# Weight pairs in arrival order for the first two x tiles, and two column halves side by side on one stationary operand

## The chip, the cores and the metric

The kernel runs on one core of one Trainium2 chip. The metric is the time of one execution in device microseconds (us). Before the change the median was 496.4 us in three runs.

## The reference

Two attention blocks read the same x (2048 rows, 1024 columns, bf16) and are mixed by a gate for each row. Block A is linear attention, block B attends to 8 positions, each 2 apart.

```
g = sigmoid((x * gate_w).sum(-1))
A: phi(t) = where(t > 0, t + 1, exp(t)) + 1e-6          # 32 heads of 32
   kv = sum_s phi(k) v ;  z = sum_s phi(k) ;  o = phi(q) kv / (phi(q) z + 1e-6) ;  a = o @ A_wo
B: softmax over offsets 0, 2, .. 14 of q.k * 32**-0.5 ;  o = attn v ;  b = o @ B_wo
out = g * a + (1 - g) * b
```

The kernel computes block A's kv through G = x^T phi(k): the V projection of block A is never made. It goes through these stages, in this order on TensorE (PE): warm-up, transposes of the first two x tiles, key projection with phi (`pk_ps`), G (`g_ps`), KV and z (`kv_ps`), V of block B with q of block A (`p_ps`), k and q of block B with its attention (`kq_ps`), the rest of q of block A with the last attention (`q_ps`), the output (`d_ps`). PE's order is fixed by the program; the other engines are scheduled by the toolchain.

## The kernel before

The start. The first two tiles of x are loaded as whole rows by the ACT queue, the first half of the key weights in four parts by the sync queue (SP). The other 14 tiles are transposed by the DMA on their way in.

```python
load_rows(nc.scalar, 0, 1)
load_rows(nc.scalar, 1, 2)
WkA = load_w("WkA", A_wqkv, D, "wa", parts=4, only=(0,))
for t in range(2, NB):
    nc.sync.dma_start_transpose(out=xT[:, :, t * P:(t + 1) * P], in_=rows(x, t * P, (t + 1) * P))
# ... other loads, masks ...
for i in range(5):                       # warm-up: 20 matmuls of 128 columns
    warm = ps_1.tile([P, 512], F32, name="warm", tag="p1")
    for j in range(4):
        nc.tensor.matmul(warm[:, j * P:(j + 1) * P], lhsT=onesb[:], rhs=onesb[:], start=True, stop=True)
for t in range(2):
    tp = ps_1.tile([P, KT, P], BF16, name="xt_ps", tag="p1")
    for kt in range(KT):
        nc.tensor.transpose(out=tp[:, kt, :], in_=xrow[:, t, kt * P:(kt + 1) * P], identity=ident[:])
    nc.vector.tensor_copy(out=xT[:, 0:4, t * P:(t + 1) * P], in_=tp[:, 0:4, :])
    nc.scalar.copy(out=xT[:, 4:8, t * P:(t + 1) * P], in_=tp[:, 4:8, :])
for half in range(2):
    for t in range(NB):
        pj = ps_1.tile([P, 512], F32, name="pk_ps", tag="p1")
        for kt in range(KT):
            nc.tensor.matmul(pj[:], lhsT=xT[:, kt, t * P:(t + 1) * P], rhs=WkA[half][:, kt, :], ...)
        phi(pk[:, t, half * 512:(half + 1) * 512], pj)
```

G, V, q and the output all have this shape: one half of 512 columns is finished before the other begins, and the stationary operand (`lhsT`) is loaded again for the second half.

```python
for half in range(2):                    # G; V, q and output likewise
    for kt in range(KT):
        pj = ps_1.tile([P, 512], F32, name="g_ps", tag="p1")
        for t in range(NB):
            nc.tensor.matmul(pj[:], lhsT=xrow[:, t, kt * P:(kt + 1) * P],
                             rhs=pk[:, t, half * 512:(half + 1) * 512], ...)
        nc.scalar.copy(out=g_[:, kt, :], in_=pj[:])
for c in range(KT):                      # KV: the first one needs G[0][:, 0..7, :]
    for kt in range(KT):
        nc.tensor.matmul(kvp[:], lhsT=WvA[c // 4][:, kt, ...], rhs=G[c // 4][:, kt, ...], ...)
```

The attention writes `Ob`, of which there are two buffers, and a transposing DMA empties it. The output of tile 0 uses banks of the attention's PSUM pools, tiles 1 to 15 use a pool that takes over those banks.

```python
Ob = small.tile([P, 4, 4, Dh], BF16, name="Ob", tag="Ob")      # pool of 2 buffers
# ...
interleave(list(out_units(0, bank8)), carry)                   # tile 0: banks of ps_o and ps_pj
with ExitStack() as s3:
    ps_3 = s3.enter_context(tc.tile_pool(name="ps_3", bufs=6, space=bass.MemoryType.PSUM))
    for t in range(1, NB):                                     # tiles 1 to 15
        ...
```

Of the kernel before, what the change touches and what calls it, by code (L numbers as in the profile page):

```python
# [8 lines left out]
ACT = mybir.ActivationFunctionType  # L9
ALU = mybir.AluOpType  # L10
BF16 = mybir.dt.bfloat16
# [3 lines left out]
P = 128  # L15
# [26 lines left out]
def kernel(  # L42
# [38 lines left out]

    def load_w(name, src, col0, tag, parts=1, only=(0, 1)):
        halves = []
        for h in only:
            w = wpool.tile([P, KT, 512], BF16, name=f"{name}{h}", tag=tag)
            c0 = col0 + h * 512
            n = KT // parts
            for i in range(parts):
                nc.sync.dma_start(
                    out=w[:, i * n:(i + 1) * n, :],  # L90
                    in_=src[i * n * P:(i + 1) * n * P, c0:c0 + 512].rearrange("(kt p) n -> p kt n", p=P))
            halves.append(w)
        return halves
# [4 lines left out]
    def load_rows(eng, t0, t1):  # L98
        eng.dma_start(out=xrow[:, t0:t1, :], in_=rows(x, t0 * P, t1 * P).rearrange("(t p) d -> p t d", p=P))

    load_rows(nc.scalar, 0, 1)
    load_rows(nc.scalar, 1, 2)
    WkA = load_w("WkA", A_wqkv, D, "wa", parts=4, only=(0,))
    for t in range(2, NB):
# [40 lines left out]
    def phi(dst, pj):  # L145
        e = work.tile([P, 512], F32, name="e", tag="e")
        nc.scalar.activation(out=e[:], in_=pj[:], func=ACT.Exp)  # L147
        nc.vector.tensor_scalar(out=e[:], in0=e[:], scalar1=1.0, scalar2=1e-6, op0=ALU.min, op1=ALU.add)  # L148
        nc.vector.scalar_tensor_tensor(out=dst, in0=pj[:], scalar=0.0, in1=e[:], op0=ALU.max, op1=ALU.add)

    with tc.manual_schedule(engines={PE}):

        with ExitStack() as s1:
# [4 lines left out]
            for i in range(5):  # L158
                warm = ps_1.tile([P, 512], F32, name="warm", tag="p1")
                for j in range(4):  # L160
                    nc.tensor.matmul(warm[:, j * P:(j + 1) * P], lhsT=onesb[:], rhs=onesb[:], start=True, stop=True)
            for t in range(2):
                tp = ps_1.tile([P, KT, P], BF16, name="xt_ps", tag="p1")
                for kt in range(KT):
                    nc.tensor.transpose(out=tp[:, kt, :], in_=xrow[:, t, kt * P:(kt + 1) * P], identity=ident[:])
                nc.vector.tensor_copy(out=xT[:, 0:4, t * P:(t + 1) * P], in_=tp[:, 0:4, :])
                nc.scalar.copy(out=xT[:, 4:8, t * P:(t + 1) * P], in_=tp[:, 4:8, :])

            s1.enter_context(tc.manual_schedule(engines={DVE}))
            pk = big.tile([P, NB, D], BF16, name="pk", tag="pkO")  # L170
            for half in range(2):
                for t in range(NB):
                    pj = ps_1.tile([P, 512], F32, name="pk_ps", tag="p1")
                    for kt in range(KT):
                        nc.tensor.matmul(pj[:], lhsT=xT[:, kt, t * P:(t + 1) * P], rhs=WkA[half][:, kt, :],  # L175
                                         start=(kt == 0), stop=(kt == KT - 1))
                    phi(pk[:, t, half * 512:(half + 1) * 512], pj)
            zacc = junk.tile([P, D], F32, name="zacc", tag="zacc")
            gw_row = junk.tile([P, D], BF16, name="gw_row", tag="gw")
            nc.gpsimd.dma_start(out=gw_row[:], in_=gate_w.partition_broadcast(P))  # L180
            zhl = junk.tile([P, 2, D], BF16, name="zhl", tag="zhl")
# [8 lines left out]

            G = []
            for half in range(2):
                g_ = kq.tile([P, KT, 512], BF16, name=f"G{half}", tag="kq")
                G.append(g_)
                for kt in range(KT):
                    pj = ps_1.tile([P, 512], F32, name="g_ps", tag="p1")
                    for t in range(NB):
                        nc.tensor.matmul(pj[:], lhsT=xrow[:, t, kt * P:(kt + 1) * P],  # L198
                                         rhs=pk[:, t, half * 512:(half + 1) * 512],
                                         start=(t == 0), stop=(t == NB - 1))  # L200
                    nc.scalar.copy(out=g_[:, kt, :], in_=pj[:])
                    side(half * 8 + kt)

# [48 lines left out]

            def v_units(t):
                def mm(half, kt, st):
                    if kt == 0:
                        st["pj"] = bank1()
                    nc.tensor.matmul(st["pj"][:], lhsT=xT[:, kt, t * P:(t + 1) * P], rhs=WvB[half][:, kt, :],  # L257
                                     start=(kt == 0), stop=(kt == KT - 1))
                    if kt < KT - 1:
                        return  # L260
                    v = Vst[t % 2]
                    nc.scalar.copy(out=v[:, half * 16:(half + 1) * 16, 0:Dh],  # L262
                                   in_=st["pj"][:].rearrange("p (h e) -> p h e", h=16))
                    if half == 1:
                        par, j = divmod(t, 8)

                        n = 128 - 16 * j
                        nc.sync.dma_start(out=V[16 * j:128, par * 9 + j], in_=v[0:n])
                        nc.sync.dma_start(out=V[0:16 * (j + 1), par * 9 + j + 1], in_=v[128 - 16 * (j + 1):128])
                for half in range(2):  # L270
                    st = {}
                    for kt in range(KT):
                        yield lambda half=half, kt=kt, st=st: mm(half, kt, st)

            def normalize(t, pq, pn, prod):
# [10 lines left out]

            def qa_units(t, bank, evacuate):
                def mm(half, kt, st):
                    if kt == 0:
                        st["pj"] = bank()  # L290
                    nc.tensor.matmul(st["pj"][:], lhsT=xT[:, kt, t * P:(t + 1) * P], rhs=WqA[half][:, kt, :],  # L291
                                     start=(kt == 0), stop=(kt == KT - 1))
                    if kt == KT - 1:
                        evacuate(t, half, st["pj"])
                for half in range(2):
                    st = {}
                    for kt in range(KT):
                        yield lambda half=half, kt=kt, st=st: mm(half, kt, st)

            def qa_finish(t, half, pj):  # L300
# [5 lines left out]

            units = [u for t in range(4) for u in v_units(t)]
            interleave(units, [(4 + 8 * c, w2_event(c)) for c in range(KT)])
            for t in range(12):
                for u in v_units(4 + t):  # L310
                    u()
                for u in qa_units(t, bank1, qa_finish):
                    u()
# [3 lines left out]
        with ExitStack() as s2:  # L317
# [125 lines left out]
            def out_units(tb, bank):  # L443
                def mm(c0, n, side, c, st):
                    if side == 0 and c == 0:
                        st["ps"] = bank()
                    if side == 0:
                        lhsT, W = (pqT[0][:, c, tb * P:(tb + 1) * P] if tb < 4 else
                                   pqT[1][:, c, (tb - 4) * P:(tb - 3) * P]), WoA
                    else:  # L450
                        lhsT, W = OBT[:, c, tb * P:(tb + 1) * P], WoB
                    nc.tensor.matmul(st["ps"][:, 0:n], lhsT=lhsT, rhs=W[c0 // 512][:, c, c0 % 512:c0 % 512 + n],  # L452
                                     start=(side == 0 and c == 0), stop=(side == 1 and c == KT - 1))
                    if side == 0 or c < KT - 1:
                        return
                    osb = work.tile([P, 512], BF16, name="osb", tag="e")
                    nc.scalar.activation(out=osb[:, 0:n], in_=st["ps"][:, 0:n], func=ACT.Copy,  # L457
                                         scale=omg[:, tb:tb + 1])
                    nc.sync.dma_start(out=rows(out2, tb * P, (tb + 1) * P)[:, c0:c0 + n], in_=osb[:, 0:n])
                parts = [(0, 512), (512, 512)] if tb < NB - 1 else [(0, 512), (512, 256), (768, 256)]  # L460
                for c0, n in parts:
                    st = {}
                    for side in range(2):
                        for c in range(KT):
                            yield lambda c0=c0, n=n, side=side, c=c, st=st: mm(c0, n, side, c, st)

# [8 lines left out]
            ev = carry + attention_events(KT - 1, prev, CUTS3, 3, 17)  # L475
            interleave([u for t in range(12, 16) for u in qa_units(t, bank8, qa_keep)], [e for e in ev if e[0] < 64])
            carry = [(p - 64, f) for p, f in ev if p >= 64]
# [46 lines left out]
```

## Time and profile before

| | before |
|---|---|
| median of six runs | 496.32 us (495.89 to 496.88) |
| span of the profiled run | 493.9 us |
| PE busy | 481.6 us, 98% |
| chain of waits, share of PE | 96% |

The first fence shows the busy line of the kernel before: engine, busy us (share of the span), number of instructions. PEld is the weight load of TensorE, which overlaps PE.

```profile
PE 481.6 (98%) x3276; PEld 230.1 (47%) x3336; DVE 283.4 (57%) x550; ACT 182.0 (37%) x281; POOL 8.6 (2%) x29
```

PE is all but always busy, so only what moves PE counts. The next question is whether weight loads cost PE time. The kernel before has one place where two matmuls in a row share a stationary operand, KVT with the two halves of WoA. This is its group (line, engine, operation, number, duration of one in ns, first and last start):

```profile
L246 PEld LDWEIGHTS <-KVT x16: 97/98/98, 123.0 to 138.3; 128*128 128x128 bf16 x16
L246 PE MATMUL p_ps<-WoA_106,KVT x8: 379/379/380, 123.2 to 138.3; 128*128 128x512 bf16 x8
L246 PE MATMUL p_ps<-WoA_108,KVT x8: 379/379/379, 123.4 to 138.5; 128*128 128x512 bf16 x8
```

There are 16 loads for 16 matmuls: a shared operand is loaded twice all the same. 379 ns is the length of one matmul, not its cost: the starts in a stream are 216 ns apart. The G stage shows it without counting records: 256 matmuls take 55.25 us, 215.8 ns each, with a load of 98 ns hidden beneath each.

The timeline of PE at the start (start us, length us, what, how many, in brackets the idle time before it and what ended it):

```profile
2.70 0.74 PE L161 MATMUL warm<-onesb 128*128 128x128 bf16 x5
4.57 1.04 PE L165 MATMUL xt_ps<-ident,xrow 128*128 128x128 bf16 x8 [1.13 <-DMA xrow<-in_A_x_dram]
5.88 1.03 PE L165 MATMUL xt_ps<-ident,xrow 128*128 128x128 bf16 x8 [0.27 <-DMA xrow<-in_A_x_dram]
6.71 5.59 PE L175 MATMUL pk_ps<-WkA_77,xT 128*128 128x512 bf16 x21
```

PE waits for the two tiles of x and then runs. The record of starts has the first key matmuls 427 ns apart, the later ones 216: the clock was at half until 8.06 us. The last view is of PE's waits (who waited for what, us in total, times, longest):

```profile
PE oB_4252 L390 <- DVE Ob L396: 1.5, 1, 1.5
PE xt_ps L165 <- DMA xrow<-in_A_x_dram: 1.4, 2, 1.1
PE kq_ps L334 <- issue: 1.3, 8, 0.2
PE warm L161 <- DVE onesb L119: 1.1, 1, 1.1
PE oB_4202 L390 <- DVE Ob L396: 0.5, 1, 0.5
```

### The profile page before, as it was taken

Reading aid. Unit: us, or ns where it says so; the run is one execution under the profiler, and the core shown is the slowest. Engines: PE = TensorE matmul, PEld = TensorE weight load, DVE = VectorE, ACT = ScalarE, POOL = GpSimd, SP = SyncE. Lnnn points to the kernel's source line nnn. Section 1 sums busy time; section 2 is a strip of 40 time slices with the busy share of each in tenths; the row PEclk is TensorE's granted clock in tenths of the full one; section 3 lists DMA queues with packets and bytes.
Section 4 is the critical chain, followed back from the end, with each engine's and each line's share of the span. In section 5 each row is a group of like instructions: output and inputs, shape, how many; then the busy total and the mean of one; then the engine's idle time right before and its main releaser. Section 6 shows DMA issues by size and latency. Waiting matters only on the chain.

```text
span 493.9 us, 8164 instructions
## 1 busy us (share of the span) xinstructions
PE 481.6 (98%) x3276; PEld 230.1 (47%) x3336; DVE 283.4 (57%) x550; ACT 182.0 (37%) x281; POOL 8.6 (2%) x29
## 2 busy tenths in 40 slices
PE   7999999999999999999999999999998999999997
PEld 4444444446444444444444444544444444444444
DVE  2666699921329999996567676767655596000000
ACT  2333311112543333331555655565564323112121
POOL 4000000001100000000000000000000000000000
PEclk9999999999999999999999999999999999999999
DMA  8999920002422122244011141111172843110101
GB/s 232 163 317 361 345 95 0 1 0 68 152 75 70 74 88 92 94 145 139 11 33 29 27 119 38 29 28 34 31 175 54 209 86 82 36 42 33 43 33 42
DMA packets 78069, 46.03 MB, mean 93 GB/s; under 512 B 51472, under 2 KB 72080, under 8 KB 78032
## 3 DMA queue, kind: packets, MB, share of 16 engines
q1 hardware_dynamic: 77664, 44.73, 32.9%
q10 hardware_dynamic: 288, 0.52, 0.4%
q8 instruction: 26, 0.43, 0.4%
q0 software_dynamic: 80, 0.26, 0.2%
q14 instruction: 11, 0.09, 0.1%
HBM read 21.23 MB, written 7.34 MB: 58 GB/s over the span
## 4 chain that ended last, share of the span: by engine, by line
PE 96%; DMA 2%; issue 1%; DVE 0%; ACT 0%; SPq 0%; ACTq 0%; DVEq 0%
PE kq_ps L334 22%; PE d_ps L452 21%; PE pk_ps L175 11%; PE g_ps L198 11%; PE p_ps L257 11%; PE p_ps L291 8%; PE q_ps L291 1%; DMA OBT<-Ob 1%; DMA xrow<-in_A_x_dram 1%; PE kv_ps L216 1%; PE q_ps_4367 L452 1%; PE p_ps L246 1%; PE q_ps L452 1%; PE q_ps_4147 L291 0%; PE q_ps_4248 L291 0%
## 5 line engine op out<-in xcount | busy, mean ns | idle before, releaser
L198 PE MATMUL g_ps<-pk,xrow 128*128 128x512 bf16 x251 | 55.2, 379 | 0.3
L457 ACT ACTIVATE osb<-d_ps,omg 128x512 bf16<-128x512 f32 (+1 forms) x31 | 20.9, 673 | 77.0 <-PE d_ps L452 72.5
L148 DVE TENSOR_SCALAR e<-e 128x512 f32<-128x512 f32 x64 | 27.2, 425 | 36.0 <-ACT e L147 35.8
L175 PEld LDWEIGHTS <-xT 128*128 128x128 bf16 x256 | 25.3, 99 | 30.4 <-issue 0.6
L452 PEld LDWEIGHTS <-OBT 128*128 128x128 bf16 x264 | 25.8, 98 | 29.2
L198 PEld LDWEIGHTS <-xrow 128*128 128x128 bf16 x256 | 25.0, 98 | 30.2
L257 PEld LDWEIGHTS <-xT 128*128 128x128 bf16 x256 | 25.0, 98 | 30.2
L291 PEld LDWEIGHTS <-xT 128*128 128x128 bf16 x256 | 24.2, 98 | 28.0
L373 DVE TENSOR_TENSOR PT_1878<-PT_1878,mask 128x672 bf16<-128x672 bf16 (+3 forms) x42 | 23.6, 571 | 17.0 <-ACT PT_1878 L371 16.7
L334 PE MATMUL kq_ps<-xT,WqB_1861 128*128 128x512 bf16 x120 | 31.8, 379 | 1.0 <-issue 0.6
L147 ACT ACTIVATE e<-pk_ps 128x512 f32<-128x512 f32 x32 | 19.1, 597 | 36.3 <-PE pk_ps L175 35.2
L334 PE MATMUL kq_ps<-xT,WqB_1859 128*128 128x512 bf16 x124 | 31.7, 379 | 0.7 <-issue 0.5
L334 PE MATMUL kq_ps<-xT,WkB_1056 128*128 128x512 bf16 x122 | 31.6, 379 | 0.2
L340 DVE CAST kqt<-kq_ps 128x512 bf16<-128x512 f32 x32 | 22.0, 687 | 16.4 <-PE kq_ps L334 16.4
L334 PE MATMUL kq_ps<-xT,WkB_1054 128*128 128x512 bf16 x120 | 30.7, 379 | 0.4 <-issue 0.2
L373 DVE TENSOR_TENSOR PT_1879<-PT_1879,mask 128x672 bf16<-128x672 bf16 (+3 forms) x40 | 22.2, 564 | 15.3 <-ACT PT_1879 L371 15.1
L257 PE MATMUL p_ps<-WvB_112,xT 128*128 128x512 bf16 x126 | 30.6, 379 | 0.1
L257 PE MATMUL p_ps<-WvB_110,xT 128*128 128x512 bf16 x125 | 30.6, 379 | 0.1
L262 ACT CAST tmp<-p_ps 128x512 bf16<-128x512 f32 x32 | 18.8, 587 | 30.3 <-PE p_ps L257 27.9
L452 PEld LDWEIGHTS <-pqT_4425 128*128 128x128 bf16 x200 | 19.6, 98 | 22.1
L175 PE MATMUL pk_ps<-WkA_77,xT 128*128 128x512 bf16 x125 | 28.3, 386 | 0.2
L452 PE MATMUL d_ps<-WoB_4065,OBT 128*128 128x512 bf16 (+1 forms) x126 | 28.3, 366 | 0.1
(400 smaller groups left out, 669.2 us busy)
## 6 DMA issues: line engine op xcount, KB each, us to landing
out_dram<-osb SPq DMA_DIRECT2D x31, 128.0 KB, 1.9
xrow<-in_A_x_dram SPq DMA_DIRECT2D x3, 1024.0 KB, 12.0
pqd<-tmp SPq DMA_DIRECT2D x12, 256.0 KB, 2.0
V<-tmp SPq DMA_DIRECT2D x4, 264.0 KB, 2.5
WkA_77<-in_A_wqkv_dram SPq DMA_DIRECT2D x4, 256.0 KB, 5.5
WkA_96<-in_A_wqkv_dram SPq DMA_DIRECT2D x1, 1024.0 KB, 7.0
WvA_102<-in_A_wqkv_dram SPq DMA_DIRECT2D x1, 1024.0 KB, 14.3
WvA_104<-in_A_wqkv_dram SPq DMA_DIRECT2D x1, 1024.0 KB, 15.2
```

The source lines that it names most:

```text
L147: nc.scalar.activation(out=e[:], in_=pj[:], func=ACT.Exp)
L148: nc.vector.tensor_scalar(out=e[:], in0=e[:], scalar1=1.0, scalar2=1e-6, op0=ALU.min, op1=ALU.add)
L175: nc.tensor.matmul(pj[:], lhsT=xT[:, kt, t * P:(t + 1) * P], rhs=WkA[half][:, kt, :], start=(kt == 0), stop=(kt == KT - 1))
L198: nc.tensor.matmul(pj[:], lhsT=xrow[:, t, kt * P:(kt + 1) * P], rhs=pk[:, t, half * 512:(half + 1) * 512], start=(t == 0), stop=(t == NB - 1))
L257: nc.tensor.matmul(st["pj"][:], lhsT=xT[:, kt, t * P:(t + 1) * P], rhs=WvB[half][:, kt, :], start=(kt == 0), stop=(kt == KT - 1))
L262: nc.scalar.copy(out=v[:, half * 16:(half + 1) * 16, 0:Dh], in_=st["pj"][:].rearrange("p (h e) -> p h e", h=16))
L291: nc.tensor.matmul(st["pj"][:], lhsT=xT[:, kt, t * P:(t + 1) * P], rhs=WqA[half][:, kt, :], start=(kt == 0), stop=(kt == KT - 1))
L334: nc.tensor.matmul(st["pj"][:], lhsT=W[c // 4][:, kt, (c % 4) * P:(c % 4 + 1) * P], rhs=xT[:, kt, cols], start=(kt == 0), stop=(kt == KT - 1))
L340: nc.vector.tensor_copy(out=kqt[:, 1, cols], in_=st["pj"][:])
L373: nc.vector.tensor_tensor(out=ptv[:, hs], in0=ptv[:, hs], in1=m[:, None, :].broadcast_to([P, 2, W_]), op=ALU.mult)
L452: nc.tensor.matmul(st["ps"][:, 0:n], lhsT=lhsT, rhs=W[c0 // 512][:, c, c0 % 512:c0 % 512 + n], start=(side == 0 and c == 0), stop=(side == ...
L457: nc.scalar.activation(out=osb[:, 0:n], in_=st["ps"][:, 0:n], func=ACT.Copy, scale=omg[:, tb:tb + 1])
```

## The change

Its intent is twofold. At the start, x arrives in two column halves of both tiles, each followed by the weights that can be used with it, all in one queue in the order of use, and the first two tiles go through the weights as a pair. In G, V, q and output the two column halves run side by side, so that each stationary operand serves two matmuls in a row. The gate weights move from the POOL queue to the sync queue. Cut to its core:

```diff
-    load_rows(nc.scalar, 0, 1)
-    load_rows(nc.scalar, 1, 2)
-    WkA = load_w("WkA", A_wqkv, D, "wa", parts=4, only=(0,))
+    WkA = [wpool.tile([P, KT, 512], BF16, name="WkA0", tag="wa")]
+    for i in range(4):
+        if i < 2:
+            nc.sync.dma_start(out=xrow[:, 0:2, i * 512:(i + 1) * 512],
+                              in_=rows(x, 0, 2 * P)[:, i * 512:(i + 1) * 512].rearrange("(t p) d -> p t d", p=P))
+        nc.sync.dma_start(out=WkA[0][:, 2 * i:2 * i + 2, :],
+                          in_=A_wqkv[2 * i * P:(2 * i + 2) * P, D:D + 512].rearrange("(kt p) n -> p kt n", p=P))
 ...
-            for t in range(2):
-                tp = ps_1.tile([P, KT, P], BF16, name="xt_ps", tag="p1")
-                for kt in range(KT):
-                    nc.tensor.transpose(out=tp[:, kt, :], ...)
+            for i in range(2):
+                for t in range(2):
+                    tp = ps_1.tile([P, 4, P], BF16, name="xt_ps", tag="p1")
+                    for j in range(4):
+                        kt = 4 * i + j
+                        nc.tensor.transpose(out=tp[:, j, :], ...)
+                    (nc.scalar.copy if t else nc.vector.tensor_copy)(
+                        out=xT[:, 4 * i:4 * i + 4, t * P:(t + 1) * P], in_=tp[:])
 ...                                   # key projection: tiles 0 and 1 as a pair, the others as before
-            nc.gpsimd.dma_start(out=gw_row[:], in_=gate_w.partition_broadcast(P))
+            nc.sync.dma_start(out=gw_row[:], in_=gate_w.partition_broadcast(P))
 ...
+            G = [kq.tile([P, KT, 512], BF16, name=f"G{half}", tag="kq") for half in range(2)]
+            for kt in range(KT):
+                pj = [ps_1.tile([P, 512], F32, name="g_ps", tag="p1") for _ in range(2)]
+                for t in range(NB):
+                    for half in range(2):
+                        nc.tensor.matmul(pj[half][:], lhsT=xrow[:, t, kt * P:(kt + 1) * P],
+                                         rhs=pk[:, t, half * 512:(half + 1) * 512], ...)
+                for half in range(2):
+                    nc.scalar.copy(out=G[half][:, kt, :], in_=pj[half][:])
+                    side(kt * 2 + half)
 ...                                   # V and q: pair_units instead of v_units, qa_units
-                parts = [(0, 512), (512, 512)] if tb < NB - 1 else [(0, 512), (512, 256), (768, 256)]
-                for c0, n in parts:
+                groups = [[(0, 512), (512, 512)]] if tb < NB - 1 else [[(0, 512)], [(512, 256)], [(768, 256)]]
+                for parts in groups:
                     st = {}
                     for side in range(2):
                         for c in range(KT):
-                            yield ...
+                            for i in range(len(parts)):
+                                yield ...
```

## The prediction

> **What bounds it now.** TensorE. The page's busy line has PE at 481.6 of 493.9 us (98%), and the chain of waits is 96% PE. Inside the long streams (key projection, G, V and q, output) the matmuls in the timeline start 216 ns apart for 512 columns. The Trainium skill ("TensorE: Matmul & The Clock Gate", Part 1, "Wait — 56ns, not 53.3ns?") gives 215.7 ns as warm back-to-back spacing, so these streams already run at the array's rate. Weight loads (98 ns each, 3336 of them, 230 us busy) lie beneath the matmuls and cost no time: the same page (Part 2, step 1) says that loads are pulled ahead of running matmuls, and the trace agrees.
>
> **The pairing itself: nothing.** The kernel already has pairs with one stationary operand: the small products of KVT with the two halves of WoA. The group for that line shows 16 weight loads for 16 matmuls, so the second load is not dropped; and their starts are 216 ns apart as everywhere. So G (256 matmuls), V (256), the early q (192) and the output (480 paired) keep 216 ns: 0 us. Weight loads should stay near 3336, PEld near 230 us.
>
> **What can move.**
> 1. Start. Now the first tile lands at 4.53 us, the second at 5.83; first key matmul at 6.71. The first three run at 427 ns, the cold rate (same page, Part 1), warm from about 8.2. No weight wait is seen after that. The new order wants 768 KB (two column halves of x and one weight part) before the second transposes; from the bytes landed in the DMA records (250 to 350 GB/s) I estimate 5.3 us, first key matmul near 6.2. If the clock is released at the same time, half of the 0.5 us goes into more cold matmuls: -0.2 to -0.6 us. The x transposes by DMA are issued about 1 us later; they had some 1.5 us to spare.
> 2. G to KV. The first KV product now needs the last chunk of G half 0, whose copy (0.58 us on ACT) starts only at the end of G: estimated +0.25 us.
> 3. V/q to k/q projection at 222 us. VectorE is at 93% in the V/q stage (window table, 18.5 of 20 us). Both phi of the last q tile now start together: VectorE is about 1 us later when it must evacuate the first q bank (CAST now 226.9 to 227.5, needed at 227.7). Up to +0.9 us, if the scheduler keeps the order; taken as +0.4.
> 4. Gate weight load moved to the sync queue, behind a load that waits to 62.8 us: VectorE's side work starts perhaps 2 us late, but it ends at 100 us and is needed at 118: 0.
> 5. Output pairs: both evacuations (0.67 us each) fall together, hidden below 6.9 us of matmuls; last tile unchanged: 0.
> 6. The 1.5 us stall at 371 us (oB waiting for VectorE and DMA) is untouched.
>
> Sum: -0.4 + 0.25 + 0.4, less a small allowance for gains at the start: 496.3 us, range 494.9 to 497.5. Faster by over 2%: 1%; within 2%: 98%; slower: 1%.
>
> **What would show it.** Spacing of 216 ns and unchanged weight-load counts in the paired groups (if loads halve and spacing falls, I am wrong); first key matmul near 6.2 us; a PE gap of a quarter of a us before the KV products; a PE gap near 227.7 us waiting for VectorE.
>
> **What would make it wrong.** Spacing below 216 ns in pairs; x transposes landing late and stalling tiles 2 to 5; a different clock release; a changed queue order that enlarges or removes the stall at 371 us.

## The result, and the profile after

The changed kernel took 497.67 us (median of six, 495.63 to 499.22) against 496.32 us (six, 495.89 to 496.88). The ratio is 1.0028 with a 95% interval of 1.0004 to 1.0053. A ratio here is the mean time of one kernel's fast runs over that of the other's of the same rounds, so it is not quite the ratio of the medians. By the means the loss is 1.4 us. The forecast class (within 2%) held; the time lies 0.17 us above the forecast range. Six more runs on another occasion gave 497.94 us and 1.0026 (1.0004 to 1.0049).

The busy line after:

```profile
PE 486.9 (98%) x3336; PEld 230.3 (46%) x3336; DVE 283.1 (57%) x550; ACT 176.8 (36%) x281; POOL 8.0 (2%) x28
```

The number of weight loads and their busy time are as before: nothing was saved there. (PE shows 3336 records instead of 3276 because fewer are missing from this trace; the program has as many matmuls as loads.) The start after:

```profile
2.69 0.74 PE L161 MATMUL warm<-onesb 128*128 128x128 bf16 x5
3.70 1.03 PE L167 MATMUL xt_ps<-ident,xrow 128*128 128x128 bf16 x8 [0.26 <-POOL mask L127]
6.32 1.03 PE L167 MATMUL xt_ps<-ident,xrow 128*128 128x128 bf16 x8 [1.58 <-DMA xrow<-in_A_x_dram]
7.14 5.13 PE L179 MATMUL pk_ps<-WkA_75,xT 128*128 128x512 bf16 x17
```

The first halves come 0.9 us earlier than the first tile did, the second halves 0.4 us later than the second tile. The program's order gives PE nothing to do between them, so it sits idle for 1.58 us, and the first key matmul is 0.4 us later. Its waits:

```profile
PE xt_ps L167 <- DMA xrow<-in_A_x_dram: 1.6, 1, 1.6
PE oB_4254 L398 <- DVE Ob L404: 1.3, 1, 1.3
PE warm L161 <- DVE onesb L119: 1.1, 1, 1.1
PE d_ps L461 <- ACT osb L466: 0.6, 1, 0.6
```

The last line is new: the output waits for the ACT engine. The timeline there, of the kernel before (ACT evacuations `osb` and the PE groups around them):

```profile
383.42 0.69 ACT L457 ACTIVATE osb<-q_ps_4367,omg 128x512 bf16<-128x512 f32 x1 [3.17 <-PE q_ps_4367 L452]
...
384.94 1.89 PE L452 MATMUL q_ps<-WoB_4065,OBT 128*128 128x512 bf16 x8
386.67 1.89 PE L452 MATMUL d_ps<-WoA_106,pqT_4069 128*128 128x512 bf16 x8
386.87 0.69 ACT L457 ACTIVATE osb<-q_ps,omg 128x512 bf16<-128x512 f32 x1 [2.77 <-PE q_ps L452]
```

and of the kernel after:

```profile
387.55 0.69 ACT L466 ACTIVATE osb<-q_ps_4369,omg 128x512 bf16<-128x512 f32 x1 [6.41 <-PE q_ps_4369 L461]
388.14 0.68 ACT L466 ACTIVATE osb<-q_ps,omg 128x512 bf16<-128x512 f32 x1
388.29 0.38 PE L461 MATMUL d_ps<-WoA_106,pqT_4071 128*128 128x512 bf16 x1 [0.56 <-ACT osb L466]
```

In the kernel before, the evacuation of `q_ps_4367`, whose bank belongs to a pool that the output stage takes over, ended 2.6 us before the new pool's first matmul. In the kernel after it begins when tile 0 ends, and the first matmul of the new pool waits for it. (The source agrees that it is a bank of the old pool: the first half of tile 0 is the ninth call of `bank8`, and each third call takes a bank of `ps_o`. And PE goes on at 388.29 us, 0.05 us after this evacuation ends at 388.24 and before the second one does.)

The third place is KV, here in the kernel before

```profile
117.89 1.78 PE L216 MATMUL kv_ps<-G_639,WvA_102 128*128 128x128 bf16 x29
118.09 0.58 ACT L201 CAST G_799<-g_ps 128x512 bf16<-128x512 f32 x1 [2.87 <-PE g_ps L198]
```

and in the kernel after:

```profile
118.93 0.59 ACT L206 CAST G_641<-g_ps 128x512 bf16<-128x512 f32 x1 [5.83 <-PE g_ps L202]
118.95 1.73 PE L221 MATMUL kv_ps<-G_641,WvA_102 128*128 128x128 bf16 x24
```

The copy that runs at the start of KV is now that of G's first half, which the eighth KV matmul needs: its start comes 286 ns after the seventh's instead of 56.

The best way to see all of it at once is a table of stages, from the start of the first matmul of a stage to the start of the first of the next, from the records of starts (us):

| stage | before | after | difference |
|---|---|---|---|
| to first key matmul | 6.71 | 7.14 | +0.43 |
| key projection | 55.93 | 56.55 | +0.62 |
| G | 55.25 | 55.25 | 0 |
| KV, z | 4.44 | 4.66 | +0.22 |
| V and q | 100.15 | 100.15 | 0 |
| k, q, attention | 136.79 | 136.79 | 0 |
| last q, attention, output tile 0 | 27.41 | 27.75 | +0.34 |
| output tiles 1 to 15 | 103.53 | 103.53 | 0 |
| after the last matmul's start | 3.71 | 3.61 | -0.10 |
| span | 493.92 | 495.43 | +1.51 |

The stages of the paired streams (G, V and q, output tiles 1 to 15), and the attention between them, are the same to 0.01 us. All of the loss is at seams. The key projection can be worked out from the starts and the clock record. Its 256 matmuls take 55.25 us at the full clock; to that comes half of the time from the first key matmul to the release of the clock, since a matmul at half clock takes 427 ns instead of 216. For the kernel before that is (8.06 - 6.71) / 2 = 0.68 us, for the kernel after, whose clock was released at 9.76 us, (9.76 - 7.14) / 2 = 1.31 us. So the +0.62 us are time at half clock. In all eight looks (a look is one profiled run) of this case in which the release came once, after the first key matmul, and nothing else fell into the stage, this sum is right to 0.03 us. The stage with output tile 0 contains the new wait (0.56 us idle) and an old wait for Ob that differs from run to run.

### The profile page after: what moved, and what is told of

Its sections match the earlier page's. It is cut to its first block, busy times and chain, and to the rows that moved or that the text cites. A ratio compares the mean times of both kernels' runs of the same rounds, so it can differ in the third digit from the quotient of the medians.

```text
span 495.4 us, 8209 instructions
## 1 busy us (share of the span) xinstructions
PE 486.9 (98%) x3336; PEld 230.3 (46%) x3336; DVE 283.1 (57%) x550; ACT 176.8 (36%) x281; POOL 8.0 (2%) x28
## 4 chain that ended last, share of the span: by engine, by line
PE 97%; DMA 2%; ACT 0%; SPq 0%; issue 0%; DVE 0%; ACTq 0%; DVEq 0%
PE kq_ps L342 23%; PE d_ps L461 21%; PE p_ps L264 20%; PE pk_ps L179 11%; PE g_ps L202 11%; PE q_ps L276 2%; DMA OBT<-Ob 1%; DMA xrow<-in_A_x_dram 1%; PE q_ps_4369 L461 1%; PE p_ps L251 1%; PE kv_ps L221 1%; PE q_ps L461 1%; PE q_ps_4149 L276 0%; PE q_ps_4250 L276 0%; ACT osb L466 0%; PE xt_ps L167 0%
## 5 line engine op out<-in xcount | busy, mean ns | idle before, releaser
L264 PEld LDWEIGHTS <-xT 128*128 128x128 bf16 x448 | 43.8, 98 | 52.9
L264 PE MATMUL p_ps<-WvB_110,xT 128*128 128x512 bf16 x128 | 48.5, 379 | 0.0
L264 PE MATMUL p_ps<-WvB_112,xT 128*128 128x512 bf16 x128 | 48.5, 379 | 0.0
L466 ACT ACTIVATE osb<-d_ps,omg 128x512 bf16<-128x512 f32 (+1 forms) x31 | 19.4, 670 | 73.6 <-issue 53.2
L461 PE MATMUL d_ps<-WoB_4067,OBT 128*128 128x512 bf16 (+1 forms) x128 | 44.5, 366 | 0.0
L461 PE MATMUL d_ps<-WoB_4065,OBT 128*128 128x512 bf16 x120 | 44.3, 379 | 0.0
L179 PEld LDWEIGHTS <-xT 128*128 128x128 bf16 x256 | 25.4, 99 | 30.9 <-issue 1.7
L264 PE MATMUL p_ps<-WqA_114,xT 128*128 128x512 bf16 x96 | 36.4, 379 | 0.0
L264 PE MATMUL p_ps<-WqA_116,xT 128*128 128x512 bf16 x96 | 36.4, 379 | 0.0
L461 PE MATMUL d_ps<-WoA_108,pqT_4427 128*128 128x512 bf16 (+1 forms) x104 | 35.4, 363 | 0.0
L461 PE MATMUL d_ps<-WoA_106,pqT_4427 128*128 128x512 bf16 x96 | 35.2, 379 | 0.0
L381 DVE TENSOR_TENSOR PT_1880<-PT_1880,mask 128x672 bf16<-128x672 bf16 (+3 forms) x42 | 23.6, 572 | 16.9 <-ACT PT_1880 L379 16.6
L342 PE MATMUL kq_ps<-xT,WkB_1058 128*128 128x512 bf16 x128 | 32.9, 380 | 0.0
L342 PE MATMUL kq_ps<-xT,WqB_1863 128*128 128x512 bf16 x128 | 32.9, 379 | 0.0
L342 PE MATMUL kq_ps<-xT,WkB_1056 128*128 128x512 bf16 x128 | 32.3, 379 | 0.0
L342 PE MATMUL kq_ps<-xT,WqB_1861 128*128 128x512 bf16 x128 | 32.2, 379 | 0.0
```

Source lines behind the costliest of these rows:

```text
L179: nc.tensor.matmul(pj[i][:], lhsT=xT[:, kt, t * P:(t + 1) * P], rhs=WkA[half][:, kt, :], start=(kt == 0), stop=(kt == KT - 1))
L264: nc.tensor.matmul(pj[half][:], lhsT=xT[:, kt, t * P:(t + 1) * P], rhs=W[half][:, kt, :], start=(kt == 0), stop=(kt == KT - 1))
L342: nc.tensor.matmul(st["pj"][:], lhsT=W[c // 4][:, kt, (c % 4) * P:(c % 4 + 1) * P], rhs=xT[:, kt, cols], start=(kt == 0), stop=(kt == KT - 1))
L381: nc.vector.tensor_tensor(out=ptv[:, hs], in0=ptv[:, hs], in1=m[:, None, :].broadcast_to([P, 2, W_]), op=ALU.mult)
L461: nc.tensor.matmul(st[i][:, 0:n], lhsT=lhsT, rhs=W[c0 // 512][:, c, c0 % 512:c0 % 512 + n], start=(side == 0 and c == 0), stop=(side == 1 ...
L466: nc.scalar.activation(out=osb[:, 0:n], in_=st[i][:, 0:n], func=ACT.Copy, scale=omg[:, tb:tb + 1])
```

## The experiments

The following theory was tested. S (start): the new order delivers the second halves late, PE idles, and its clock is released late and at a varying time. E (ends of pairs): KV and the pool change each wait for an evacuation that pairing moved to the end. The rivals: the paired streams themselves cost something; or the spread of the times comes from the stall at `Ob` in the middle.

The times of all runs (median, range, ratio to the kernel before of the same rounds with its 95% interval):

| run | what | us | ratio |
|---|---|---|---|
| e1_start_only | before + new start | 497.25 (496.5 to 499.74) | 1.0025 (1.0005 to 1.0045) |
| e2_pairs_only | after, old start | 496.69 (496.51 to 497.38) | 1.0007 (0.9995 to 1.0018) |
| e3_after_fill | after + 20 warm-up matmuls | 496.82 (495.8 to 499.72) | 1.0016 (0.9993 to 1.0039) |
| e4_before_fill | before + 16 warm-up matmuls | 494.91 (494.78 to 495.05) | 0.9967 (0.9955 to 0.9979) |
| e5_after_ob4 | after, 4 Ob buffers | 495.46 (494.74 to 495.75) | 0.9982 (0.997 to 0.9994) |
| e6_after_xact | after, x on ACT queue | 498.56 (497.47 to 498.87) | 1.0046 (1.0034 to 1.0058) |
| e7_after_serial_ends | after, last of G and first output tile serial | 496.29 (494.78 to 497.78) | 1.0002 (0.9983 to 1.0022) |
| e8_best | before + warm-up + 4 Ob | 492.86 (492.83 to 493.16) | 0.9935 (0.9923 to 0.9946) |
| e9_after_interleave | after, key matmuls between transposes | 497.32 (495.62 to 498.29) | 1.001 (0.9984 to 1.0036) |
| e10_best_interleave | interleaved start in the best kernel | 493.68 (493.46 to 493.89) | 0.994 (0.9916 to 0.9963) |
| e11_after_again | after | 497.94 (497.42 to 498.71) | 1.0026 (1.0004 to 1.0049) |
| e12_after_look | after, one run | 498.49 | - |
| e13_after_mended | after, all faults out | 492.74 (492.67 to 492.89) | 0.9931 (0.9917 to 0.9944) |
| e14_best_again | as e8_best | 493.02 (492.82 to 493.17) | 0.9936 (0.9923 to 0.9948) |
| e15_before_look | before, one run | 497.01 | - |
| e16_rows_one_queue | before, whole rows in the new order | 497.48 | - |

All gave correct results. A caution about spreads: in the rounds of e9 to e11 the kernel before itself ran from 494.85 to 499.06 us (eleven runs), where its range in the other four sets was 1.0 to 1.8 us; and the six runs of e11_after_again lie within 1.3 us, where the first six of the same kernel spread over 3.6. So a wide spread does not belong to the new start alone, and five or six runs show it poorly. From each profile, the start of G tells how the start of the kernel went (it holds the landing, the cold matmuls and any stall); "Ob" is the stage of last q, attention and output tile 0:

| profile | x complete | clock full from | G starts | KV stage | Ob stage |
|---|---|---|---|---|---|
| before | 5.83 | 8.06 | 62.64 | 4.44 | 27.41 |
| e15_before_look | 6.21 | 9.96 | 63.76 | 4.44 | 27.60 |
| e2_pairs_only | 6.04 | 9.02 | 63.22 | 4.66 | 27.79 |
| after | 6.27 | 9.76 | 63.69 | 4.66 | 27.75 |
| e11_after_again | 6.46 | 9.44 | 63.63 | 4.66 | 27.81 |
| e12_after_look | 6.55 | 11.49 | 64.69 | 4.66 | 27.92 |
| e7_after_serial_ends | 6.81 | 11.99 | 65.08 | 4.44 | 27.04 |
| e5_after_ob4 | 6.63 | 4.21, half from 7.62, full from 11.03 | 64.07 | 4.66 | 25.77 |
| e1_start_only | 6.18 | 4.78 | 63.57 | 4.44 | 26.96 |
| e3_after_fill | 6.16 | 6.66 | 62.15 | 4.66 | 30.55 |
| e4_before_fill | 6.02 | 4.70 | 62.14 | 4.44 | 27.07 |
| e8_best | 5.89 | 6.74 | 62.15 | 4.44 | 25.05 |
| e13_after_mended | 6.02 | 4.54 | 62.15 | 4.44 | 25.05 |
| e14_best_again | 6.23 | 5.35 | 62.48 | 4.44 | 25.05 |
| e6_after_xact | 6.63 | 11.93 | 64.95 | 4.66 | 27.81 |
| e9_after_interleave | 6.48 | 10.63 | 64.32 | 4.66 | 27.86 |
| e10_best_interleave | 6.21 | 7.14 | 62.73 | 4.44 | 25.05 |
| e16_rows_one_queue | 5.91 | 9.26 | 64.45 | 4.44 | 27.10 |

("x complete": last of the 16 completion marks of the second load of x; "clock full from": the clock records. The profile is one of the timed runs; its time is the span plus 1.7 to 2.1 us in all of them.)

### The start alone, and the pairs alone

e1_start_only is the kernel before with the new start: the first two hunks of the diff above and the first two tiles as a pair. e2_pairs_only is the kernel after with these undone (the gate weights stay on the sync queue).

> The kernel before with only the new start (column halves of x and weight parts in arrival order on one queue, first two tiles as a pair), nothing else paired. Theory A (the loss is at the start: second column halves land at 6.3 us instead of tile 2 at 5.8, and the clock is released later, 9.8 instead of 8.1 us): 0.6 to 1.3 us slower than before, a spread of several us between runs, first key matmul near 7.1 us. Rival B (the paired streams cost the time, the start nothing): within 0.2 us of before, spread as before.

> The kernel after with the old start. Theory A: 0.4 to 0.6 us slower than before: a gap of 0.23 us in the first KV product (seventh to eighth matmul) and one of about 0.7 us before the first output group after the pool change, waiting for the ACT evacuation; all paired matmuls 216 ns apart; spread narrow as before, about 1 us. Rival B: about 1.4 us slower, as the whole change.

The start alone cost 1.2 us by its ratio, with the wide spread; the pairs alone 0.35 us by theirs, with an interval that reaches from -0.25 to 0.9 us, and a spread of 0.9 us. So S holds for most of the loss. The wide spread (3.2 us) came with the new start here, but see the caution above and the run with four Ob buffers below: whose it is stays open. In e2_pairs_only the KV stage was 4.66 us and the wait of the output for ACT was there, 0.6 us idle, as E says. But e1_start_only got there in another way than expected. Its clock was at full from 4.78 us, and the first key matmul came at 6.69, yet it lost the gain again:

```profile
3.66 1.04 PE L167 MATMUL xt_ps<-ident,xrow 128*128 128x128 bf16 x8 [0.22 <-POOL mask L127]
6.23 0.62 PE L167 MATMUL xt_ps<-ident,xrow 128*128 128x128 bf16 x8 [1.54 <-DMA xrow<-in_A_x_dram]
6.69 3.62 PE L179 MATMUL pk_ps<-WkA,xT 128*128 128x512 bf16 x15
11.76 1.47 PE L179 MATMUL pk_ps<-WkA,xT 128*128 128x512 bf16 x6 [1.45 <-DMA xT<-in_A_x_dram]
```

PE waited 1.45 us for x tile 2, whose transposing DMA landed at 11.7 us instead of 9.3. In e1_start_only the gate weights are still loaded by POOL, as in the kernel before, and they landed between 9.3 and 11.5 us. In e16_rows_one_queue, with POOL as well, tile 2 landed at 12.6 us and PE waited 1.0 us; in the looks in which x and weights came in one queue and the gate weights did not use POOL it landed by 9.9 us, at 9.41 in the kernel after. So with the new order of loads the move of the gate weights does not look neutral: the two looks without it had a stall, those with it had none. That POOL's load is the cause was not tried by itself.

### Warm-up

```diff
-            for i in range(5):
+            for i in range(6):                         # e4_before_fill: range(8)
                 warm = ...
             for i in range(2):
+                for _ in range(4 if i else 0):          # e4_before_fill: 1, before the second tile
+                    warm = ...                          # four matmuls of 128 columns
                 for t in range(2):
                     ... transposes ...
```

> The kernel after with 20 more warm-up matmuls: 4 before the first transposes, 16 between the two column halves, where PE sits idle 1.9 us. If the late release of the clock causes the spread and part of the loss: release before the first key matmul or at most one or two cold key matmuls, 0.8 to 1.5 us faster than the kernel after, spread below 1.5 us. If the late landing alone costs: less than 0.4 us gained and the spread stays. The first key matmul stays near 7.1 us or 0.4 us earlier (transposes at the full clock).

> The kernel before with 16 more warm-up matmuls (12 before the first tile lands, 4 between the two tiles). If the clock counts at the start: released at or before the first key matmul, so three to four cold key matmuls of 427 ns become 216 ns: 0.4 to 1.0 us faster than before, spread no wider. If not: within 0.2 us of before.

For the kernel before, the 16 matmuls that compute nothing gained 1.6 us by the ratio and narrowed the spread to 0.3 us; more than expected. G started at 62.14 us, 0.5 to 1.6 us earlier than in the three looks with the old start. For the kernel after, G started at 62.15 us, 1.5 us earlier than in its first look, as the clock theory has it. Yet its times were hardly better and their spread remained. The profile fell on a slow run, 498.6 us, and showed why: the middle. These are the windows of it (busy time of each engine, then the granted clock, the DMA share and GB/s):

```profile
365.00:370.00 5.00, 4.70 (x53) 1.96 (x52) 1.74 (x6) 2.97 (x5) 0.00 (x0) 1.00 0.82 209
370.00:375.00 5.00, 2.36 (x26) 0.97 (x27) 1.92 (x5) 1.34 (x3) 0.00 (x0) 1.00 0.66 115
375.00:380.00 5.00, 4.73 (x48) 2.10 (x49) 2.02 (x5) 2.40 (x5) 0.00 (x0) 0.66 0.16 32
```

PE stood idle for 2.6 us at 371 us, waiting for Ob, which waited for the transposing DMA; 1.6 us after PE had resumed, the clock went to half for 3.4 us (375.3 to 378.7). The stage took 30.55 us. So the rival theory of the middle is right as well, at least for this slow run.

### The stall in the middle

```diff
+            obp = s2.enter_context(tc.tile_pool(name="obp", bufs=4))
-                    Ob = small.tile([P, 4, 4, Dh], BF16, name="Ob", tag="Ob")
+                    Ob = obp.tile([P, 4, 4, Dh], BF16, name="Ob", tag="Ob")
```

> The kernel after with four buffers instead of two for the attention output Ob, so that VectorE need not wait for the transposing DMA at 365 to 375 us. In one look that took 2.6 us of PE idle and set the clock to half for 3.4 us. Theory M (the spread of the kernel after comes from this stall in the middle): no PE wait for Ob there, 1.5 to 2.5 us faster than the kernel after, spread below 1.2 us. Rival S (the spread comes from the start, late landings of the first tiles): the stall is gone too and about 1.5 us are gained, but the spread stays at 3 us.

> The kernel before with the longer warm-up (16 more matmuls) and four Ob buffers. Warm-up alone gave 494.9. With the stall at 371 us gone too: 492.8 to 493.8, 0.5 to 0.7% faster than before, spread below 1 us. If the wait only moves to the next thing (transposes land late for the output instead), about 494.9 as with the warm-up alone.

With four buffers no wait for Ob is left, the stage takes 25.77 us in the kernel after and 25.05 in the kernel before, 2 us less in each. e5_after_ob4 never went over 495.75 us, and its five runs lie within 1.0 us. By its own expectation that is theory M: 2.2 us gained between the medians and a spread below 1.2 us, with the new start still in place. So the wide spread of the kernel after is not the start's alone; what part each has, these few runs do not settle. Its profile showed the second way in which the start costs time:

```profile
0.00:5.00 5.00, 3.22 (x28) 2.78 (x28) 1.07 (x7) 1.77 (x2) 4.33 (x24) 1.00 0.50 143
5.00:7.60 2.60, 0.93 (x11) 0.69 (x12) 0.43 (x1) 0.37 (x2) 0.00 (x0) 1.00 1.12 337
7.60:11.00 3.40, 3.40 (x10) 1.18 (x9) 0.00 (x0) 0.32 (x1) 0.00 (x0) 0.50 1.18 206
11.00:15.00 4.00, 3.95 (x19) 1.80 (x19) 2.05 (x4) 1.68 (x3) 0.00 (x0) 1.00 1.06 159
```

Here the clock had been released at 4.21 us. PE then idled for the second halves, and at 7.62 us the clock fell back to half for 3.4 us, just after the key matmuls had begun (7.13 us). (In the first two windows the column says 1.00 also where no record stands; the starts 107 ns apart for 128 columns show that PE ran at half until 4.2.)

e8_best, the kernel before with both mends, ran in 492.86 us: 0.65% less than before, and within 0.33 us in all its runs.

### The queue of the x halves

```diff
-            nc.sync.dma_start(out=xrow[:, 0:2, i * 512:(i + 1) * 512],
+            nc.scalar.dma_start(out=xrow[:, 0:2, i * 512:(i + 1) * 512],
```

> The kernel after with the two column halves of x issued on the ACT queue, beside the weight parts, instead of in one queue with them. If the queueing behind the first weight part makes the second halves late: they land near 5.5 us instead of 6.2, first key matmul 0.5 to 0.8 us earlier, up to 0.8 us gained. If the sharing of the DMA engines does: within 0.3 us of the kernel after at the start.

This missed: the second halves landed at 6.63 us, not earlier, the first at 4.79 us instead of 3.65, and the kernel was no faster. In this one look, then, leaving the one queue did not help. e16_rows_one_queue made the opposite test, whole rows in the queue and order of the change:

```diff
-    load_rows(nc.scalar, 0, 1)
-    load_rows(nc.scalar, 1, 2)
-    WkA = load_w("WkA", A_wqkv, D, "wa", parts=4, only=(0,))
+    for i in range(4):
+        if i < 2:
+            load_rows(nc.sync, i, i + 1)
+        ... weight part i on nc.sync ...
```

> The kernel before with its two x tiles as whole rows (packets of 2 KB) put into the one queue in the order of the change (tile 0, first weight part, tile 1, other parts). The column halves of the change (packets of 1 KB, same bytes before them) landed at 3.5 to 4.2 and 6.2 to 6.8 us. If the smaller packets are slow: here the second lands at 5.9 us or earlier. If the one queue is: at 6.2 us or later.

The second tile landed at 5.91 us. (The kernel gained nothing by it: tile 2 was late, as told above, and G started at 64.45 us.) Over all looks, x in whole rows (packets of 2 KB) was complete at 5.83 to 6.23 us (eight looks, both arrangements of queues), x in column halves (packets of 1 KB) at 6.16 to 6.81 (ten looks, both arrangements). The medians are 6.02 and 6.47; the ranges touch, and each of the two crossed arrangements has one look. The shape of the load goes with a delay of about 0.4 us; by what mechanism no run shows. The Trainium skill ("DMA: Bandwidth & Descriptors", Specifications) gives 512 B and more as enough for the line rate. By 6.27 us all DMA engines together had moved 1129 KB in the kernel before and 1133 KB in the kernel after. So the delay is one of this load, not of the rate.

What goes with the queue is how far apart the 16 completion marks of the second load of x come (the load has landed with the last of them): 1.26 to 1.99 us in the ten looks with x and weights in one queue, e16_rows_one_queue (1.56) among them, and 0.44 to 0.80 us in the eight with x on the ACT queue, e6_after_xact (0.60) among them.

### The ends of the pairs

```diff
-                for t in range(NB):
-                    for half in range(2):
+                for t, half in ([(t, h) for t in range(NB) for h in range(2)] if kt < KT - 1 else
+                                [(t, h) for h in range(2) for t in range(NB)]):
 ...
-                groups = [[(0, 512), (512, 512)]] if tb < NB - 1 else ...
+                groups = [[(0, 512)], [(512, 512)]] if tb == 0 else [[(0, 512), (512, 512)]] if tb < NB - 1 else ...
```

> The kernel after with the last chunk of G and the first output tile serial, half by half, all other pairs kept. The 0.23 us gap in the first KV product and the 0.7 us gap before the first output group of the last stage both go, everything else unchanged: 0.7 to 0.9 us faster than the kernel after in the stage table (KV stage back to 4.4 us, q stage near 27.0 to 27.4), spread of the kernel after kept. If the pairs elsewhere cost something, the streams of G, V and q, and output are longer than in before by more than 0.1 us each.

Both waits went: KV took 4.44 us again, and the stage with output tile 0 took 27.04. With two Ob buffers that stage takes 26.96 to 27.60 us in the six profiles with a serial tile 0 (mean 27.20) and 27.75 to 27.92 in the six with a paired one (mean 27.82; the disturbed 30.55 is left out), so the pool change cost 0.6 us net, with a wait of 0.56 us idle in the profile. The streams of G, V and q and output kept their lengths. The spread of 3 us stayed, and its slow profile (497.8 us) had G start at 65.08 us with the middle undisturbed: here the slow run goes with a late start.

### PE's order at the start

```diff
-            for i in range(2):
+            def turn_rows(i):
                 for t in range(2):
                     ... transposes of column half i ...
 ...
                     for kt in range(KT):
+                        if half == 0 and t0 == 0 and kt % 4 == 0:
+                            turn_rows(kt // 4)
                         for i in range(n):
```

> The kernel after, with the key matmuls of chunks 0 to 3 put between the transposes of the first and of the second column half, so that PE need not hold the first key matmul for the second halves (they landed at 6.2 to 6.9 us in all looks with the new start). If PE's program order wasted the arrival order: first key matmul at 4.9 to 5.9 us (when the first weight part lands, 5.0 to 5.9), G starts at 62.0 to 63.2 instead of 63.7 to 65.1 us, 0.8 to 2 us faster than the kernel after. If a landing of weights or of the next x tile (9.4 us) then limits: a PE wait shows there and under 0.5 us is gained.

> The streams of before, the interleaved start of the run beside it with 12 more warm-up matmuls, the gate weights on the sync queue, four Ob buffers. e8_best had G start at 62.15 us and 492.9 us. If the start is now bound by the first weight part and the clock is released by 4.2 to 6.7 us: G starts at 61.0 to 62.0, time 491.8 to 492.8. If x tile 2 (landing at 9.4 to 9.9) binds: about as e8_best, 492.6 to 493.4.

In e9_after_interleave the first key matmul came at 5.89 us, as expected, waiting for the first weight part. But the clock was released at 10.63 us in this look, so PE ran the first eight at half speed, and G started at 64.32 us, where 62.0 to 63.2 was expected. Nothing was gained beyond the interval. In e10_best_interleave the same order with warm-up started the key matmuls at 5.63 us, and still G started at 62.73 us, no earlier than in e8_best, and the time of 493.68 us missed both of its expected ranges: the clock came at 7.14, the copy of the second halves cost a further wait of 0.3 us. Its ratio, 0.994, cannot be told from e8_best's 0.9935. In these two looks an earlier start was worth little while the clock was at half.

### The kernel after again, and before again

> The kernel after, unchanged, for its spread and a second look. Start theory: the first-key time plus cold and stalled time of the key stage (G start, 63.7 us in the first look) varies between looks by over 1 us, with the landing of the second column halves (6.2 to 6.9) and the release of the clock (4.2 to 12 us). Middle theory: G start stays within 0.3 us of 63.7, and slow runs show a q stage over 29 us with the clock at half for 3.4 us. Median 497 to 498.5, range 3 us.

> A third look at the kernel after, for the same question as the run before it: start (G start apart from 63.7 us by up to 1.5 us) or middle (q stage over 29 us).

> A second look at the kernel before. G started at 62.64 us in the first, whose time was 0.6 us below the mean of all runs. If the start of before also varies with the clock's release: G start anywhere from 62.1 to 63.9. If it does not: 62.6 plus or minus 0.2. In the five looks with the new start it was 63.6 to 65.1.

The two further looks at the kernel after took 497.42 and 498.49 us, 1.07 us apart; G started at 63.63 and 64.69 us, 1.06 us apart. The middle was the same in sum (164.71 us from the start of k and q to the end of tile 0 in both). The expected range of 3 us missed: the six runs lie within 1.3. In the second look at the kernel before G started at 63.76 us. The old start gives 62.64, 63.22 and 63.76 (mean 63.2), the new one 63.63 to 65.08 in five looks (mean 64.2; the kernel after three times, e5 and e7, all with the gate weights on the sync queue): it costs about 1.0 us. That is a mean of few, and the looks are not drawn evenly from all runs; the order of size is what is shown.

### The pairs with the faults out

e13_after_mended is the kernel after with the old start, the warm-up of e4_before_fill, four Ob buffers and the serial ends of e7_after_serial_ends. e14_best_again is e8_best, on the same chip.

> The kernel after with the old start, the longer warm-up, four Ob buffers, and its last G chunk and first output tile serial: all that was found to cost time taken out, the pairs of G, V, q and output kept. If the pairs cost and gain nothing: every stage as in the best kernel beside it within 0.05 us (G 55.25, KV 4.44, V and q 100.15, output 103.53), total within 0.3 us of it, 492.6 to 493.4. If the pairs cost something not yet seen: over 0.5 us slower than it.

> The kernel before with the longer warm-up and four Ob buffers, a second time, on the same chip as the one above: 492.6 to 493.4, spread below 1 us.

492.74 and 493.02 us. Every stage after the start is equal to 0.01 us (G 55.25, KV 4.44, V and q 100.15, k and q 136.79, Ob 25.05, output 103.53); G starts 0.33 us apart and the time after the last matmul's start differs by 0.14 us, 3.59 against 3.73. The pairs of 1120 matmuls (224 of G, 448 of V and q, 448 of the output), with a stationary operand shared two by two, gain and cost nothing on PE. The lines of this kernel and of the other beside it have the same count of loads, here e13_after_mended:

```profile
PE 481.6 (98%) x3291; PEld 230.8 (47%) x3352; DVE 283.9 (58%) x550; ACT 177.3 (36%) x281; POOL 7.9 (2%) x28
```

and e14_best_again:

```profile
PE 481.8 (98%) x3291; PEld 231.1 (47%) x3352; DVE 283.8 (58%) x550; ACT 182.0 (37%) x281; POOL 8.6 (2%) x29
```

## Why the prediction was right or wrong

The range missed the median by 0.17 us, on the slow side. The terms of the prediction's sum, one by one:

- **The pairing itself, 0 us: right.** The lengths of G, V with q, and the output stream are the same to 0.01 us, and the loads are 3336 in both. What the Trainium skill says ("TensorE: Matmul & The Clock Gate", Part 2, step 1), that loads are pulled ahead of running matmuls, agrees: 98 ns of load are hidden beneath each 215.8 ns.
- **1, the start, -0.2 to -0.6 us: wrong, and the main miss.** It was about +1.0 us, in the profiled pair +1.05 (0.43 to the first key matmul, 0.62 in the key stage). The step that failed is "I estimate 5.3 us, first key matmul near 6.2". The second halves landed at 6.27 us and the key matmul came at 7.14. The estimate divided the bytes by the mean rate of all DMA engines. The bytes did move at that rate (791 KB of the queue's loads by 5.3 us, where 768 KB were wanted), but a load has landed only with the last of its 16 completion marks, and those of the second halves came from 5.01 to 6.27 us; in the kernel before, those of the second tile came from 5.36 to 5.83. The other failed step is the condition "If the clock is released at the same time". It was released at 9.76 us instead of 8.06, and the cold time accounts for the 0.62 us in the key stage. Why it came later is not shown. PE's hole before the second transposes had grown from 0.27 to 1.58 us, but the release varies with either start: 8.06 to 9.96 us in three looks with the old one, 4.21 to 11.99 with the new one, and in e1_start_only, with a hole of 1.54 us, it came at 4.78. The x transposes by DMA stalled nothing in the kernel after, as said.
- **2, G to KV, +0.25 us: right**, +0.22 us (the gap is 286 ns instead of 56).
- **3, k and q projection at 222 us, +0.4 us: 0.** VectorE was indeed late, by 0.8 us: its product with `zrow` started 2.02 us after the stage's first matmul in the kernel before (224.49, stage from 222.47) and 2.86 us after it in the kernel after (226.62, stage from 223.76). Absolute times do not compare here, since the stage itself starts 1.3 us later. Behind the reduction of 1.2 us the evacuation (CAST) would have ended near 229.6 us, an estimate from these durations, and the bank was wanted at 228.94. But the scheduler put it ahead of that reduction, and PE did not wait. The timeline of VectorE shows the two orders, in the kernel before

```profile
224.49 1.22 DVE L276 TENSOR_TENSOR tmp<-tmp,zrow 128x1024 f32<-128x1024 bf16 x1
225.75 1.22 DVE L278 TENSOR_REDUCE den<-tmp 128x32 f32<-128x1024 f32 x1
226.88 0.68 DVE L340 CAST kqt<-kq_ps 128x512 bf16<-128x512 f32 x1
```

and in the kernel after:

```profile
226.62 1.22 DVE L297 TENSOR_TENSOR tmp<-tmp,zrow 128x1024 f32<-128x1024 bf16 x1
227.76 0.68 DVE L348 CAST kqt<-kq_ps 128x512 bf16<-128x512 f32 x1
228.36 1.21 DVE L299 TENSOR_REDUCE den<-tmp 128x32 f32<-128x1024 f32 x1
```

The condition that the prediction named ("if the scheduler keeps the order") did not hold.
- **4, gate weights, 0: right for the kernel as it is.** The KV stage shows no other wait than that of point 2. But leaving them on POOL with the new loads went with a stall of 1.0 to 1.5 us in the two looks that had it.
- **5, output pairs, 0: wrong**, about +0.6 us. Hidden below 6.9 us of matmuls are the evacuations of tiles 1 to 14. The failing step is the one for tile 0, which the prediction took with them: its evacuation lies at a change of PSUM pools, and the next pool's first matmul waits for it. e7_after_serial_ends took this wait away by that edit, together with that of point 2.
- **6, the stall at 371 us, untouched: right on the mean, but it was not harmless.** It varies, and in one profile (e3_after_fill) half clock for 3.4 us followed it.

In sum: +1.0 (start) +0.2 (KV) +0.6 (pool change) -0.1 (tail) is 1.7 us, against 1.4 us between the means of the timed runs, whose interval is 0.2 to 2.6 us. The predicted sum had +0.25.

The profile would have told the fifth point ahead of time: the evacuation of `q_ps_4367` at 383.42 us, of the old pool, ended 2.6 us before the first `d_ps`, and the change moved it behind tile 0's last matmul.

## What to carry to other kernels

When weight loads are already hidden and streams run at the array's spacing, pairing matmuls on one stationary operand moves nothing but the evacuations, which gather at the end of a pair; look at each seam (next stage, next pool, next consumer) for one that now waits. At the start of a kernel, the clock of TensorE can be worth more than the order of arrival: bridge the waits for the first data with matmuls that compute nothing (here -1.6 us for 16 of them in the kernel before; in the kernel after 20 of them brought G forward by 1.5 us in the one look, its times by less than the noise). When a load is estimated, look at when its last completion mark comes and not only at the bytes. A wait in the middle can cost twice, by itself and by the half clock that follows, so a third and fourth buffer of a kilobyte a partition for what a DMA empties may be worth 2 us.

## What the Trainium skill lacked or had wrong

- "TensorE: Matmul & The Clock Gate", Part 1, says that the clock falls back after an idle window of about 3.4 us, and the table of its last part asks for no idle gaps over about 3 us. Here a shorter one sufficed: 2.6 us of idle PE at 371 us (e3_after_fill) was followed by half clock from 375.3 to 378.7. (The same part does tell of a kernel that fell back through short idle times between groups of matmuls, but not how short.) In e5_after_ob4 half clock from 7.62 to 11.03 followed a hole of 2.2 us before the second halves; this case is less clear, since between the last warm-up (3.12) and the first key matmul (7.13) PE made only transposes, of which the page's Part 4 says that they do not count as busy in the same way. The lengths, 3.41 us each, agree with the window of 3413 ns that it gives.
- The same part calls the release variable from run to run, and this agrees: full from 8.06, 9.02 and 9.96 us for one start, from 4.21 to 11.99 for another. The table of the last part names a warm-up only for benchmarks. In a whole kernel, warm-up without a long hole made the release earlier and the times steadier: 4.54 to 6.74 us in the five profiles of e3, e4, e8, e13 and e14, and a spread of the times of 0.2 to 0.35 us in those four of them whose middle was undisturbed (three of the four also had four Ob buffers; e4_before_fill, 0.27 us, had not).
- The same page, "Back-to-back issue gap", says that streams of load and matmul pairs run at about 131 ns for 512 columns and 81 ns for 128. Here streams with a load for each matmul run at 215.8 ns for 512 (G) and 56 ns for 128 (KV), which are the page's own figures without loads.
- The same page, Part 4, says that the full clock does not engage for transposes, which do not count as busy in the same way. In e1_start_only, with the clock released, eight transposes started 56 ns apart; at half clock 107. So they do run at the full clock; whether they count towards its release no run shows.
- "TensorE: Matmul & The Clock Gate", Part 2, step 1, says that the separate load lets one load serve many matmuls. No page says that this toolchain does not make use of it: a stationary operand that is used twice in a row is loaded twice, with 16 loads for 16 matmuls in pairs, and 3336 loads before and after.
- No page gives how far apart the 16 completion marks of one load come. Here it was 0.44 to 0.80 us for 256 KB of x on a queue of its own, and 1.26 to 1.99 us in one queue with the weights. Nor does one give the delay by the shape of a load: the same bytes in packets of 1 KB instead of 2 KB were complete at 6.16 to 6.81 us instead of 5.83 to 6.23.
